# A SwiGLU output product by Strassen's scheme in a fused DeltaNet and FFN kernel

## The chip, the core and the metric

The kernel runs on one core of a Trainium2 chip. The metric is the device time of one execution in microseconds, lower is better. A core has five engines, each with its own in-order queue: TensorE (PE, matmuls, with the weight load PEld beside it), VectorE (DVE), ScalarE (ACT), GpSimd (POOL) and SyncE (SP, which issues most transfers). They wait for one another by semaphores. SBUF is the on-chip memory; PSUM has eight banks of 128 x 512 fp32 numbers, which matmuls write and VectorE and ScalarE read.

## The reference

Two blocks follow one another. The first is a DeltaNet recurrence over q, k, v of shape 4 x 8 x 768 x 48 (batch, heads, tokens, head width); the second is a SwiGLU feed-forward net on 3072 tokens of width 384 with 1536 hidden columns.

```python
k_n = k / (np.linalg.norm(k, axis=-1, keepdims=True) + 1e-06)
for t in range(S):
    kt, vt, bt = (k_n[:, :, t], v[:, :, t], beta[:, :, t, None])
    y[:, :, t] = np.einsum('bhd,bhde->bhe', q[:, :, t], state)
    v_old = np.einsum('bhde,bhd->bhe', state, kt)
    state = state + bt[:, :, :, None] * np.einsum('bhd,bhe->bhde', kt, vt - v_old)
# x: y as (tokens, heads * width)
rms = np.sqrt(np.mean(x * x, axis=-1, keepdims=True) + 1e-06)
xn = x / rms * rms_g
g = xn @ w_gate
silu = g * (1.0 / (1.0 + np.exp(-g)))
val = xn @ w_val
return (silu * val @ w_out).astype(np.float32)
```

Weights arrive as 64-bit floats and are turned into fp32 on the chip, with work on VectorE, ScalarE and, for the first nine of them, TensorE.

## The kernel before

The 768 tokens are cut into 12 chunks of 64; with four batches a chunk has 256 tokens for the feed-forward net. Per chunk the work is in three parts.

- *prep*: normalised keys are turned (L379) and multiplied with themselves (scores, L402, into kk through L500); the blocks go to DRAM and back into `at`, GpSimd scales and combines them (L519, L543, L553, L548), and fifteen solver steps on VectorE (`step`, L565 and L571) invert 32 x 32 triangles inside `acc`. ScalarE copies the result into `x` (L588), GpSimd a turned one into `xtr` (L592), and both go through DRAM into `mt`, `x2bd` and `m1bd`; two matmul groups (`merge1` L646 into `zz`, `merge2` L668) join two triangles into `mt`.
- *recur*: `ks` (L706) and VectorE's subtraction (L714) give `r`, `mr` (L739) gives `u` (L790, L792), `qs` (L752) and `pu` (L769) give the output, `ku` (L872) the update that VectorE adds to the state `sbd` (L881). The output is normalised into `yn` (L812, root on GpSimd L822, L827), turned (`xtr`, L837), scaled into `xf` (L840), and seven VectorE additions (L858) form sums of its blocks. `qpart` prepares the masked scores `pt`: ScalarE copies them (L445), GpSimd multiplies with the mask (L446).
- *ffn*: chunks 0 and 1 use `ffn_plain` (up L920, down L902). From chunk 2 on the gate and value products are 15 block products per half of the hidden columns instead of 18 (L1013), with weight sums made once by `factors` (L976, L978); ScalarE copies (L1025) or VectorE adds (L1023) collect them, then silu (L1029) and the product with the value (L1030) give `hf`, the 1536 hidden columns for 256 tokens. The output product runs over all 12 blocks of `hf` for both halves of tokens: 24 matmuls of 384 columns into two banks (`down_mm`, L902). `finish` copies both banks to `o_buf` (L894), and four transfers store them.

Python plans the order of the whole program ahead. `P.add` takes each operation with its engine, an estimated duration, a priority and the buffers that it reads and writes; `P.run` lets the ready operation that can start first go next, and among equals the lower priority value. Priorities come from `due(c, lead)`, a due time per chunk that moves by `PERIOD`. TensorE work of prep and recur is put ahead of the net's by `P.lead`. The order so found is each engine's queue, and the hardware keeps it whatever the real durations are. While TensorE would be idle in the first 70 us of the plan, a filler of matmuls without use is inserted (L1083).

Of the kernel before, what the change touches and what calls it, by code (L numbers as in the profile page):

```python
# [16 lines left out]
C = 64  # L17
W = 32
DP = 64
ENGINES = ("PE", "ACT", "DVE", "POOL", "SP")  # L20
# [16 lines left out]
class Plan:  # L37
# [3 lines left out]
    def __init__(self):  # L41
        self.ops, self.wrote, self.read, self.slack, self.lead = [], {}, {}, 0.0, 0.0

    def add(self, eng, dur, fn, prio, r=(), w=(), lat=0.15, ps=(), last=()):
# [11 lines left out]
        op.ahead, op.n = ahead, len(self.ops)  # L56
# [12 lines left out]
    def run(self, free, filler=None, until=0.0):  # L69
        at = dict.fromkeys(ENGINES, 0.0)  # L70
        cand = {e: [] for e in ENGINES}
        for op in self.ops:
            if not op.left:
                cand[op.eng].append(op)
        done, server = 0, 0.0
# [46 lines left out]
def kernel(  # L122
# [51 lines left out]
    o_buf = sbt("o_buf", [128, 768])  # L174
# [4 lines left out]
    NK, NKQ, NKK, NMT = 2, 2, 2, 2  # L179
# [8 lines left out]
    kk = sbt("kk", [128, 16, C], NKK)  # L188
# [4 lines left out]
    x = sbt("x", [128, W // 2, W])  # L193
    xt_ = sbt("xtr", [128, W, W // 2])
    m1bd = sbt("m1bd", [128, 16, 2, W])
    x2bd = sbt("x2bd", [128, 8, 4, W])
    zz = sbt("zz", [128, 4, 2, W])
    mt = sbt("mt", [128, 16, C], NMT)
# [5 lines left out]
    yn = sbt("yn", [128, 2, DM])  # L204

# [5 lines left out]
    sil = [tmp[:, a, 0:TOK] for a in range(2)]  # L211
# [3 lines left out]
    cvb = [o_buf, more[:, 4608:5376]]  # L215
    o_sb = o_buf.rearrange("p (two n) -> p two n", two=2)
# [19 lines left out]
    PERIOD = 54.5  # L236
# [6 lines left out]
    def setup():  # L243
# [32 lines left out]
        for i in range(NMT):  # L276
            P.add("POOL", 1.0, lambda t=mt[i]: nc.gpsimd.memset(t, 0.0), 1, w=[("mt", i, h_, bb) for h_ in range(3) for bb in range(2)] + [("mt", i, h_, bb, g) for h_ in range(2) for bb in range(2) for g in range(2)])

    def load_small():
        for i in range(8):  # L280
            src = beta.rearrange("b (y g) (c i t) -> i g (b y) c t", i=2, g=2, t=W)[i // 2 % 2, i % 2]
            dma(beta_b[16 * i : 16 * i + 16], src, 0.5, w=[("beta", i)], work=0.2)
        dma(g_sb, moe_rms_g.rearrange("(t p) -> p t", p=128), 1, w=["g"], after=30.0)


    def weights():
        todo = []
        for half_ in range(2):
# [6 lines left out]
            for f in range(6 * half_, 6 * half_ + 6, 2):  # L295
                src = moe_w_out[f * 128 : f * 128 + 256, :].rearrange("(a p) c -> p a c", a=2)
                todo.append((wo_sb[:, f : f + 2].rearrange("p a c -> p (a c)"), src, [("wo", f), ("wo", f + 1)]))
        for n, (dst, src, keys) in enumerate(todo):
# [7 lines left out]
            cc = cvb[a]  # L306

# [25 lines left out]
            P.add("DVE", 0.56, s4, pr, r=[("cvw", n)], w=[("o", a)])  # L333
            P.add("DVE", 0.97, s5, pr, r=[("raw", i)], w=[("o", a)])
            done = []
            if n < NPE:
                for x_ in range(2):
# [7 lines left out]
                    P.add("PE", 1.5, s6, pr, r=[("o", a), ("cvw", n), "ident"], w=[("cvp", n, x_)], ps=ps)  # L345
                    done.append(("cv", n, x_))
                    P.add("ACT", 0.48, lambda dst=dst[:, cols], ps=ps: nc.scalar.copy(dst, ps.t[:, 0:384]), pr, r=[("cvp", n, x_), ("cvw", n)], w=[done[-1]], last=ps)
            else:
                done.append(("cv", n))
                P.add("DVE", 0.97, lambda dst=dst, cc=cc: nc.vector.tensor_tensor(out=dst, in0=dst, in1=cc, op=ALU.add), pr, r=[("o", a)], w=[("cvw", n), done[-1]])  # L350
# [100 lines left out]
    def prep(c):  # L451
# [7 lines left out]
        i2, ikq, ikk, imt = c % 2, c % NKQ, c % NKK, c % NMT  # L459
# [5 lines left out]
        kkall = [("kk", ikk, d) for d in range(2)]  # L465
# [32 lines left out]
        for d in range(2):  # L498
            if c or d == 0:
                P.add("ACT", A(512), lambda d=d, ps=ps: nc.scalar.mul(kk[ikk][:, d:16:2], heads(ps[d]), -1.0), pr, r=[ps[d]], w=[("kk", ikk, d)], last=ps[d])  # L500
            else:
                P.add("DVE", V(512), lambda d=d, ps=ps: nc.vector.tensor_scalar_mul(kk[ikk][:, d:16:2], heads(ps[d]), -1.0), pr, r=[ps[d]], w=[("kk", ikk, d)], last=ps[d])

        kb, kbkeys = (kk[ikk], kkall) if c else (kraw, [("kr", d) for d in range(2)])
        dk = dkk[c % 2]
        for g in range(2):
            for i in range(2):
                r0 = 64 * g + W * i
                src = kb[r0 : r0 + W, :, W * i : W * i + W]
# [28 lines left out]

        diag = at_.rearrange("p j t -> p (j t)")[:, 1 : 1 + 66 * 15 + 1 : 66]
# [17 lines left out]
        P.add(e_, 0.69 if early else 1.3, share1, pi, r=[("at", 0), ("at", 1)], w=["x"])  # L557
        P.add(e_, 0.5, share3, pi, r=[("at", 0), ("at", 1)], w=["acc"])
        P.add(e_, 0.69 if early else 1.3, share2, pi, r=["x"], w=[("at", 0), ("at", 1)])
# [30 lines left out]
        P.add("ACT", 0.8, lambda: spread(x, nc.scalar.copy, False), pi, r=["acc"], w=["x"])  # L590
        if not early:
            P.add("POOL", 1.2, lambda: spread(xt_, lambda d, t: nc.gpsimd.tensor_copy(out=d, in_=t), True), pi, r=["acc"], w=["xtr"])  # L592
        q_ = "SP" if c else "ACT"
        for par in range(2):
            dst = dx[i2].rearrange("i g x (s two) t -> two (i g x) s t", two=2)[par]
            dma(dst, x[64 * par : 64 * par + 64], pi, r=["x"], w=[("dx", i2, par)], dur=0.63, work=1.0, eng=q_)
# [3 lines left out]
            dma(dst, xt_[64 * par : 64 * par + 32], pi, r=["xtr"], w=[("dxt", i2, par)], dur=0.65, work=1.0)  # L600
# [42 lines left out]
        def merge1():  # L643
            for b in range(B):
                for y_ in range(4):
                    nc.tensor.matmul(  # L646
                        ps1.t[W * y_ : W * y_ + W, 64 * b : 64 * b + 64],
                        kk[ikk][:, 4 * b + y_, W:C],
# [3 lines left out]
        P.add("PE", 0.7, merge1, pi, r=kkall + [("m1bd", g, bb) for g in range(2) for bb in range(2)], w=[ps1, "zz"], ps=ps1)  # L652
        if early:
            P.add("ACT", A(256), lambda: nc.scalar.copy(zz.rearrange("p b g s -> p (b g s)"), ps1.t[:, 0:256]), pi, r=[ps1], w=["zz"], last=ps1)
        else:
# [4 lines left out]
            ), pi, r=[ps1], w=["zz"], last=ps1)  # L660
# [13 lines left out]
        P.add("PE", 1.1, merge2, pi, r=["zz"] + [("x2bd", y_) for y_ in range(4)], w=ps2 + [("mt", imt, 2, bb) for bb in range(2)], ps=ps2)  # L674
# [10 lines left out]
    def recur(c):  # L685
        pr = due(c, 40)
        py = due(c, 30)
        ikq, imt, i2 = c % NKQ, c % NMT, c % 2
# [116 lines left out]
        px = py if c < 2 else due(c, 16)  # L805
        xdst, xkeys = (xp1, [("x1", p) for p in range(2)]) if c == 1 else (xf, [("xp", p) for p in range(2)])
        for h in halves:
# [24 lines left out]
            for p in h:  # L832
# [12 lines left out]
                ), px, r=[psx, "g"], w=[xkeys[p]], last=psx)  # L845
        if c > 1:
            X = lambda a, n, step=1: xf[:, a : a + step * (n - 1) + 1 : step]
            for dst, a, b_, op, n in (
# [11 lines left out]
                ), px, r=[("xp", 0)], w=["xc", ("xp", 1)])  # L860
# [25 lines left out]
    def finish(c, po, f0, f1):  # L886
        for p in range(2):
# [3 lines left out]
            if f0:  # L891
                P.add("DVE", V(384), lambda p=p: nc.vector.tensor_tensor(out=o_sb[:, p], in0=part[c][:, p], in1=po[p].t[:, 0:DM], op=ALU.add), -1, r=["po"] + partkeys[c], w=[("ob", p)], last=po[p])
            else:
                P.add("ACT", A(384), lambda p=p: nc.scalar.copy(o_sb[:, p], po[p].t[:, 0:DM]), -1, r=["po"], w=[("ob", p)], last=po[p])  # L894
            for bb in range(2):
                tok = (2 * bb + p) * S + c * C
                dma(out[tok : tok + C, :], o_sb[64 * bb : 64 * bb + 64, p], -1, r=[("ob", p)], w=[("out", c, p, bb)])

    def down_mm(po, f, f0, f1):
        def mm():  # L900
            for p in range(2):
                nc.tensor.matmul(  # L902
                    po[p].t[:, 0:DM], hf[:, f, 128 * p : 128 * p + 128], wo_sb[:, f], start=(f == f0), stop=(f == f1 - 1),
# [5 lines left out]
    def ffn_plain(c, f0, f1, start):  # L909
# [3 lines left out]
        def up(f):  # L913
            ps = Group()
            h_, i_, n = f // 6, f % 6 // 2, 128 * (f % 2)
            for side, key in enumerate(("wg", "wv")):
# [8 lines left out]
                P.add("PE", 1.31, mm, start + 3.9 * (f - f0), r=xk + [("wuse", h_)] + ready[(key, h_)], w=[ps, (("tmp", f % 2), ("hf", f, 0))[side]], ps=ps)  # L925
            a = f % 2
            P.add("ACT", A(256), lambda ps=ps: nc.scalar.activation(out=sil[a], in_=ps.t[:, 0:TOK], func=ACTF.Silu), -1, r=[ps], w=[("tmp", a)], last=ps)
            P.add("DVE", V(256), lambda ps=ps: nc.vector.tensor_tensor(out=hf[:, f], in0=sil[a], in1=ps.t[:, TOK : 2 * TOK], op=ALU.mult), -1, r=[("tmp", a), ps], w=[("hf", f, 0), ("hf", f, 1)], last=ps)

        def down(f):  # L930
            if f == f0:
                P.add("PE", 0.0, lambda: None, start, r=xk + [("cvp", n, x_) for n in range(NPE) for x_ in range(2)], w=["po"], ps=po[1])
            P.add("PE", 1.31, down_mm(po, f, f0, f1), start + 3.9 * (f - f0) + 9, r=[("hf", f, 0), ("hf", f, 1)] + ready[("wo", f)], w=["po"], ps=po[0])
# [66 lines left out]
    def ffn(c, start):  # L1000
        n = 0
        for h in range(2):
            ps = [Group() for _ in range(3)]
            for m, ((kind, slot), xs, b_, begin, o, more_, end) in enumerate(PRODUCTS):
# [21 lines left out]
                if end:  # L1026
# [4 lines left out]
                        out=hf[:, f0 : f0 + 2, 128 * p : 128 * p + 128],  # L1031
# [3 lines left out]
        po = [Group(), Group()]  # L1035
# [81 lines left out]
```

## Time and profile before

| what | value |
|---|---|
| median of 3 runs | 762.07 us (762.03 to 762.45) |
| profiled execution, its own time | 761.53 us |
| its span | 759.8 us |
| PE busy, share | 742.2 us, 98% |
| DVE busy, share | 528.9 us, 70% |
| ACT busy, share | 291.9 us, 38% |
| POOL busy, share | 194.1 us, 26% |
| gate and value matmuls, L1013 | 304.6 us |
| output matmuls, L902 | 197.1 us |

The span runs from the first to the last instruction that the profile shows; the execution's time has some 1.7 us around it. Busy time is a union, and matmuls are pipelined, so the mean duration of one matmul is longer than the spacing of two in a row; the chain that ended last shows spacings. PE is busy from 130.1 us on without an idle stretch up to the last output matmul. A fp32 matmul is two records in the profile.

### The profile page before, as it was taken

The numbers are of one execution on the slowest core, as the hardware profiler recorded it, in microseconds if no ns is written. First come the engines' busy times: TensorE is split into PE (matmuls) and PEld (weight loads), VectorE is DVE, ScalarE is ACT, GpSimd is POOL, SyncE is SP. The second block draws the span as 40 slices with busy tenths as digits, with TensorE's granted clock in tenths as the row PEclk, the third lists the DMA queues.
The fourth block names the chain that finished last, engine by engine and source line by source line (L and its number), as shares of the span: only waits on it lengthen the run. The fifth ranks groups of instructions, "written<-read, shape, count | busy, mean of one in ns | idle before, by whom it ended". The sixth has DMA issues, their size and how long they took to land.

```text
span 759.8 us, 21394 instructions
## 1 busy us (share of the span) xinstructions
PE 742.2 (98%) x9178; PEld 621.2 (82%) x9178; DVE 528.9 (70%) x1051; ACT 291.9 (38%) x698; POOL 194.1 (26%) x197
## 2 busy tenths in 40 slices
PE   9999995999999999999999999999999999999997
PEld 8877774877789789789699699699699699698894
DVE  4999999993865875865865865865955955944360
ACT  3425444123334334344344344344344254234230
POOL 5102206033222232332233233223323313200000
PEclk9999998999999999999999999999999999999999
DMA  7848386042352242242252252251251341120000
GB/s 169 211 88 239 108 221 154 1 70 45 63 91 45 44 79 55 43 83 52 43 89 47 43 92 43 44 92 43 49 86 44 58 77 44 21 51 3 21 2 21
DMA packets 206991, 54.55 MB, mean 72 GB/s; under 512 B 199216, under 2 KB 202288, under 8 KB 206896
## 3 DMA queue, kind: packets, MB, share of 16 engines
q1 hardware_dynamic: 201552, 52.19, 32.6%
q10 hardware_dynamic: 5344, 0.98, 0.8%
q8 instruction: 72, 1.18, 0.7%
q14 instruction: 23, 0.19, 0.1%
HBM read 40.83 MB, written 12.32 MB: 70 GB/s over the span
## 4 chain that ended last, share of the span: by engine, by line
PE 87%; DVE 4%; POOL 1%; issue 1%; ACT 0%; DVEq 0%
PE bank L1013 36%; PE bank L902 25%; PE bank L920 8%; PE bank L402 3%; PE bank L379 2%; PE bank L752 2%; PE bank L706 2%; PE bank L739 2%; PE bank L769 2%; PE bank L668 2%; PE bank L872 1%; PE bank L837 1%; PE bank L646 1%; DVE acc L571 1%; PE bank L1083 1%
## 5 line engine op out<-in xcount | busy, mean ns | idle before, releaser
L1023 DVE TENSOR_TENSOR tmp<-tmp,bank 128x512 f32<-128x512 f32 x180 | 123.1, 686 | 123.6 <-PE bank L1013 101.1
L902 PE MATMUL bank<-wo_sb,hf 128*128 128x384 f32 x576 | 197.1, 490 | 0.0
L1013 PE MATMUL bank<-xf,w_in 128*128 128x128 f32 x1440 | 179.5, 276 | 0.0
L1013 PEld LDWEIGHTS bank<-xf,w_in 128*128 128x128 f32 x1440 | 169.3, 192 | 2.8 <-issue 0.4
L902 PEld LDWEIGHTS bank<-wo_sb,hf 128*128 128x128 f32 x576 | 106.0, 190 | 63.7 <-issue 0.2
L1013 PE MATMUL bank<-xf,more 128*128 128x128 f32 x960 | 125.1, 277 | 0.0
L1013 PEld LDWEIGHTS bank<-xf,more 128*128 128x128 f32 x960 | 115.8, 192 | 4.6 <-DVE tmp L1023 1.4
L1029 ACT ACTIVATE tmp<-tmp 128x256 f32<-128x256 f32 x120 | 50.1, 417 | 116.1 <-DVE tmp L1023 115.8
L1025 ACT COPY tmp<-bank 128x512 f32<-128x512 f32 x120 | 69.9, 585 | 54.6 <-PE bank L1013 50.4
L571 DVE TENSOR_REDUCE acc<-acc 128x30 f32<-128x90 f32 (+4 forms) x180 | 85.0, 472 | 6.2
L519 POOL TENSOR_TENSOR at<-at,beta_b 128x1024 f32<-128x1024 f32 x10 | 23.6, 2362 | 203.9 <-DMA at<-dkk 203.8
L1030 DVE TENSOR_TENSOR hf<-tmp 128x256 f32<-128x256 f32 x120 | 58.7, 490 | 24.2 <-ACT tmp L1029 21.8
L565 DVE TENSOR_TENSOR acc<-acc,at 128x60 f32<-128x60 f32 (+4 forms) x180 | 68.6, 381 | 5.7
L422 POOL TENSOR_TENSOR knrm<-ksum,half 128x16 f32<-128x16 f32 x12 | 36.1, 3006 | 39.4 <-DVE ksum L421 39.2
L588 ACT COPY x<-acc 128x256 f32<-128x256 f32 x24 | 10.1, 431 | 91.4 <-DVE acc L571 90.7
L920 PE MATMUL bank<-xp,w_in 128*128 128x256 f32 x144 | 35.6, 398 | 6.6 <-DVE xp L840 6.6
L1083 PE MATMUL bank<-ident 128*128 128x128 f32 x314 | 39.0, 284 | 1.4 <-POOL ident masks.py:199 1.4
L1083 PEld LDWEIGHTS bank<-ident 128*128 128x128 f32 x314 | 37.3, 198 | 2.0 <-POOL ident masks.py:199 1.4
L920 PEld LDWEIGHTS bank<-xp,w_in 128*128 128x128 f32 x144 | 28.4, 200 | 12.9 <-DVE xp L840 6.8
L446 POOL TENSOR_TENSOR pt<-pt,mask_p 128x512 f32<-128x512 f32 x20 | 28.8, 1458 | 34.3 <-ACT pt L445 34.3
L881 DVE TENSOR_TENSOR sbd<-sbd,bank 64x384 f32<-64x384 f32 x40 | 22.1, 552 | 21.2 <-PE bank L872 20.7
L592 POOL COPY xtr<-acc 128x128 f32<-128x128 f32 x40 | 16.2, 448 | 73.5 <-DVE acc L571 73.5
(136 smaller groups left out, 873.6 us busy)
## 6 DMA issues: line engine op xcount, KB each, us to landing
at<-dkk SPq DMA_DIRECT2D x23, 256.0 KB, 4.1
more<-in_moe_w_gate_dram SPq DMA_DIRECT2D x6, 768.0 KB, 5.9
q<-in_q_dram SPq DMA_DIRECT2D x24, 192.0 KB, 4.5
more<-in_moe_w_val_dram SPq DMA_DIRECT2D x6, 768.0 KB, 5.2
vt<-in_v_dram SPq DMA_DIRECT2D x24, 192.0 KB, 4.1
more<-in_moe_w_out_dram SPq DMA_DIRECT2D x6, 768.0 KB, 6.5
out_dram<-o_buf SPq DMA_DIRECT2D x48, 96.0 KB, 2.2
k<-in_k_dram SPq DMA_DIRECT2D x23, 192.0 KB, 4.0
```

The costliest lines, as they stand in the source:

```text
L422: P.add("POOL", 2.95, lambda: nc.gpsimd.tensor_tensor(out=knrm[i2], in0=ksum[i2], in1=half, op=ALU.pow), pn, r=[("ksum", i2), "half"], w=[ ...
L446: P.add("POOL", 1.3, lambda dst=dst: nc.gpsimd.tensor_tensor(out=dst, in0=dst, in1=mask_p[:, None, :].to_broadcast([128, 8, C]), op=ALU.mu ...
L565: nc.vector.tensor_tensor(out=acc[:, 1:3, 0:n, j + 2 : W].rearrange("p a i t -> p i a t"), in0=acc[:, old, 0:n, j : j + 2, None].to_broadc ...
L571: nc.vector.tensor_reduce(out=acc[:, new, 0:n, j + 2 : W], in_=acc[:, lo : lo + 3, 0:n, j + 2 : W].rearrange("p a i t -> p i t a"), axis=A ...
L902: nc.tensor.matmul(po[p].t[:, 0:DM], hf[:, f, 128 * p : 128 * p + 128], wo_sb[:, f], start=(f == f0), stop=(f == f1 - 1), skip_group_check ...
L920: nc.tensor.matmul(ps.t[:, TOK * side : TOK * side + TOK], w_in[:, side, h_, 3 * t + i_, n : n + 128], x_[:, 2 * t : 2 * t + 2].rearrange( ...
L1013: nc.tensor.matmul(g.t[:, 128 * z : 128 * z + 128], fac[:, side, 128 * f : 128 * f + 128], xf[:, xs], start=(begin and z == 0), stop=False ...
L1023: P.add("DVE", V(512), lambda t=t, g=g: nc.vector.tensor_tensor(out=t, in0=t, in1=g.t, op=ALU.add), -1, r=[g], w=[tk], last=g)
L1025: P.add("ACT", A(512), lambda t=t, g=g: nc.scalar.copy(t, g.t), -1, r=[g], w=[tk], last=g)
L1029: P.add("ACT", A(256), lambda t=t: nc.scalar.activation(out=t[:, 0:256], in_=t[:, 0:256], func=ACTF.Silu), -1, w=[tk])
L1030: P.add("DVE", V(256), lambda t=t, f0=f0, p=p: nc.vector.tensor_tensor(out=hf[:, f0 : f0 + 2, 128 * p : 128 * p + 128], in0=t[:, 0:256].re ...
L1083: nc.tensor.matmul(warm[:, 0:128], ident, ident)
```

## The change

From chunk 2 on the output product is done as a 2 x 2 block product by seven block products. `hf` is split in two halves of tokens and two of hidden columns, `w_out` in two halves of hidden rows and two of output columns. `out_factors` makes three sums of weight blocks into a new buffer `wsum` once and overwrites one block of `w_out`; `down` makes four sums of `hf` blocks on VectorE per chunk, runs the seven products of six matmuls of 192 columns in three banks, and collects them with ScalarE copies and VectorE adds. `spot` orders the blocks of `hf` so that four of six in a half are complete before the last pair.

Room for `wsum` comes from buffers that are shared or dropped: `x` and `xtr` lie inside `acc`, `zz` inside `yn`, `kk` keeps one copy of its first part and two of its second, from chunk 2 on there is one `mt`, chunk 1's `kk`, `mt` and `x` lie inside `wsum`, `o_buf` is gone (outputs go from `tmp` and `part`), and chunk-1 sums use the old places.

The planner gets a backward pass: operations marked late take their priority from the operations that use them, less their own stretched duration. `recur` is entered before `prep`, `PERIOD` is 52.5 for 54.5, prep's slack is 0.6 for 1.5, and the priorities of the scaling into `xf` and of its sums are 29 us earlier.

```diff
+STRETCH = {"PE": 1.5, "ACT": 1.5, "DVE": 1.4, "POOL": 1.2, "SP": 1.0}
...
+        for op in reversed(self.ops):
+            if op.late:
+                op.prio = min(
+                    (u.prio - (0.0 if u.eng == op.eng and not op.dma else op.lat + u.slack + 0.2) for u in op.users),
+                    default=op.prio,
+                ) - STRETCH[op.eng] * op.dur - (3.0 if op.dma else 0.0)
...
-    o_buf = sbt("o_buf", [128, 768])
-    NK, NKQ, NKK, NMT = 2, 2, 2, 2
+    NK, NKQ = 2, 2
+    wsum = sbt("wsum", [128, 3, FT // 2, DM // 2])
+    wflat = wsum.rearrange("p a f n -> p (a f n)")
-    kk = sbt("kk", [128, 16, C], NKK)
+    kk3 = sbt("kk", [128, 3, 16, W])
+    kk = [kk3[:, 0:2], kk3[:, 0:3:2], wflat[:, 0:1024].rearrange("p (i x t) -> p i x t", i=2, t=W)]
-    x = sbt("x", [128, W // 2, W])
-    xt_ = sbt("xtr", [128, W, W // 2])
+    xs_ = [acc[:, 1], wflat[:, 2048:2560].rearrange("p (i t) -> p i t", t=W), wflat[:, 2560:3072].rearrange("p (i t) -> p i t", t=W)]
+    xt_ = acc[:, 2].rearrange("p i t -> p (i t)").rearrange("p (k i) -> p k i", i=W // 2)
-    zz = sbt("zz", [128, 4, 2, W])
-    mt = sbt("mt", [128, 16, C], NMT)
+    mt = [sbt("mt", [128, 16, C]), wflat[:, 1024:2048].rearrange("p (x t) -> p x t", t=C)]
+    zz = yn[:, 0, 0:256].rearrange("p (b g s) -> p b g s", b=4, g=2)
+    o_sb = [tmp[:, 3 + p, 0:DM] for p in range(2)]
...
-    PERIOD = 54.5
+    PERIOD = 52.5
...
+    def spot(f):
+        return f // 6 * 6 + (0, 1, 4, 5, 2, 3)[f % 6]
...
+        pxv = px if c < 2 else due(c, 45)
...
-        po = [Group(), Group()]
-        for f in range(FT):
-            P.add("PE", 1.31, down_mm(po, f, 0, FT), start + 29 + 1.4 * f, r=[("hf", f, 0), ("hf", f, 1)], w=["po"] + (["acq"] if f == 0 else []), ps=po)
-        finish(c, po, 0, FT)
+        down(c, start + 27.5)
+
+    def out_factors():
+        b = lambda i, j: wo_sb[:, 6 * i : 6 * i + 6, 192 * j : 192 * j + 192]
...
+        for n, (dst, in0, in1) in enumerate((
+            (wsum[:, 0], b(0, 1), b(0, 0)),
+            (wsum[:, 1], b(1, 1), wsum[:, 0]),
+            (wsum[:, 2], b(1, 0), wsum[:, 1]),
+            (b(0, 1), b(1, 1), b(0, 1)),
+        )):
+            P.add("DVE", V(1152), lambda dst=dst, in0=in0, in1=in1: nc.vector.tensor_tensor(out=dst, in0=in0, in1=in1, op=ALU.subtract), 175.0 if n == 3 else 165.0, r=wk, w=old + ["wsum"] + (["wouse"] if n == 3 else []))
+
+    def down(c, start):
+        a = lambda i, j: hf[:, 6 * j : 6 * j + 6, 128 * i : 128 * i + 128]
...
+        s1 = xp1
+        s2 = tflat[:, 512:1280].rearrange("p (f n) -> p f n", f=6)
+        p1, u2, p5 = tmp[:, 0, 0:192], tmp[:, 0, 192:384], tflat[:, 1280:1472]
...
+                for f in range(6):
+                    nc.tensor.matmul(g.t[:, 0:192], a_[:, f], b_[:, f], start=(begin and f == 0), stop=(f == 5), skip_group_check=True)
...
+        for z0, z1 in ((0, 4), (4, 6)):
+            k = ("x1", z0 // 4)
+            sums(s1, a(1, 0), a(1, 1), ALU.add, ak(1, 0, z0, z1) + ak(1, 1, z0, z1), [k], z0, z1)
+            sums(s2, s1, a(0, 0), ALU.subtract, ak(0, 0, z0, z1) + [k], s2k, z0, z1)
+        s1k = [("x1", 0), ("x1", 1)]
+        product(x, a(0, 0), ak(0, 0), b(0, 0), True, 0)
+        snap(p1, x, [("tmp", 0)])
+        product(z_, a(0, 1), ak(0, 1), b(1, 0), True, 2)
+        add(0, 0, p1, z_, [("tmp", 0)])
+        product(y, s1, s1k, wsum[:, 0], True, 4)
+        snap(p5, y, ["p5"])
+        sums(a(1, 0), a(0, 0), a(1, 0), ALU.subtract, ak(0, 0), ak(1, 0), 0, 6)
+        product(x, s2, s2k, wsum[:, 1], False, 6)
+        snap(u2, x, [("tmp", 0)])
+        sums(s1, a(0, 1), s2, ALU.subtract, ak(0, 1) + s2k, s1k, 0, 6)
+        product(y, s1, s1k, b(1, 1), False, 8)
+        add(0, 1, u2, y, [("tmp", 0)])
+        store(0)
+        product(x, a(1, 0), ak(1, 0), b(0, 1), False, 10)
+        add(1, 1, p5, x, [("tmp", 2), "p5"])
+        product(x, a(1, 1), ak(1, 1), wsum[:, 2], False, 12)
+        P.add("ACT", A(192), lambda: nc.scalar.copy(o_sb[1][:, 0:192], x.t[:, 0:192]), -1, r=[x], w=[("tmp", 4)], last=x)
+        store(1)
...
     for c in range(NCH):
-        P.slack, P.lead = 0.0 if c < 1 else 1.5, 1000.0
-        if c + 1 < NCH:
-            prep(c + 1)
-        P.slack = 0.0 if c < 1 else 0.3
-        recur(c)
...
+        for part_ in (recur, prep):
+            P.late = c + (part_ is prep) > 1
+            if part_ is prep:
+                P.slack, P.lead = 0.0 if c < 1 else 0.6, 1000.0
+                if c + 1 < NCH:
+                    prep(c + 1)
+            else:
+                P.slack, P.lead = 0.0 if c < 1 else 0.3, 1000.0
+                recur(c)
...
+            out_factors()
         elif c > 1:
             ffn(c, due(c, 0))
```

The seven products are called P1 to P7 below in the order of the code, and the matrix of `product(x, s2, ...)` is P4.

## The prediction

> **What bounds the kernel now.** I read the engine shares first, then the busy time by stage over three steady chunks, then the chain that ended last inside one chunk, and last the VectorE and GpSimd timelines of that chunk. The engine line of the page:
>
> ```profile
> PE 742.2 (98%) x9178; PEld 621.2 (82%) x9178; DVE 528.9 (70%) x1051; ACT 291.9 (38%) x698; POOL 194.1 (26%) x197
> ```
>
> The stage table (stretch, its length, then busy us of PE, PEld, DVE, ACT, POOL) for two chunks in the middle:
>
> ```profile
> 384.83:440.64 55.81, 55.81 (x744) 47.47 (x744) 39.04 (x81) 23.57 (x57) 17.07 (x18) 1.00 0.32 61
> 440.64:496.44 55.80, 55.80 (x744) 47.46 (x744) 38.53 (x81) 23.58 (x57) 17.06 (x18) 1.00 0.33 61
> ```
>
> TensorE never waits: a steady chunk costs 55.81 us, all of it matmul. VectorE is busy 38.8 of that. The chain inside a chunk is TensorE alone:
>
> ```profile
> 384.83 8.04 PE bank L1013 x72
> ...
> 419.58 0.93 PE bank L872 x64
> 420.51 1.02 PE bank L379 x8
> 421.54 2.58 PE bank L902 x8
> 424.12 1.09 PE bank L402 x64
> 425.21 1.49 PE bank L902 x4
> 426.70 0.66 PE bank L837 x6
> 427.36 10.32 PE bank L902 x32
> ```
>
> A matmul leaves two records. 72 records of 128 columns take 8.04 us, 0.1117 each; 32 of 384 columns 10.32, 0.3225 each; elsewhere in the chain 12 of 256 columns take 2.59, 0.2158 each. A piece after the small L402 matmuls is 0.20 longer (1.49, not 1.29). VectorE in the same place:
>
> ```profile
> 414.61 1.76 DVE L1030 TENSOR_TENSOR hf<-tmp 128x256 f32<-128x256 f32 x1
> ...
> 420.56 2.27 DVE L881 TENSOR_TENSOR sbd<-sbd,bank 64x384 f32<-64x384 f32 x4 [1.28 <-PE bank L872]
> 422.87 0.22 DVE L565 TENSOR_TENSOR acc<-acc,at 128x60 f32<-128x60 f32 x1
> ...
> 426.82 0.79 DVE L565 TENSOR_TENSOR acc<-acc,at 128x240 f32<-128x240 f32 x1
> ...
> 431.86 0.41 DVE L565 TENSOR_TENSOR acc<-acc,at 128x240 f32<-128x240 f32 x1
> ...
> 437.98 1.02 DVE L840 TENSOR_TENSOR xf<-bank,g_sb 128x384 f32<-128x384 f32 x2
> 438.92 2.41 DVE L858 TENSOR_TENSOR xf<-xf 128x256 f32<-128x256 f32 x7
> ```
>
> The fifteen solver steps (L565, L571) fill 422.87 to 436.87 without a gap, exactly under the output product, which today asks nothing of VectorE. Two rows are odd: 1.76 us for a product that mostly takes 0.42, and 0.79 where the same shape takes 0.41. GpSimd explains both:
>
> ```profile
> 414.35 1.75 POOL L543 TENSOR_TENSOR x<-at 128x512 f32<-128x512 f32 x1
> ...
> 425.91 2.83 POOL L446 TENSOR_TENSOR pt<-pt,mask_p 128x512 f32<-128x512 f32 x2 [3.55 <-ACT pt L445]
> ```
>
> [...] L1030 (two SBUF inputs) ends when L543 ends, while L1023, which reads a bank, keeps 0.69 beside L519. [...] the trace has 0.686 for N=512 [...] and 0.957 for 768 [...]
>
> **The change, part by part.** *Output product.* Before, 24 matmuls of 384 columns: 48 x 0.3225 = 15.48 us. After, seven products P1 to P7 of six matmuls of 192 columns: 84 records. No row has 192 columns; the middle of 128 and 256 is 0.1638 [...]. 84 x 0.1638 = 13.76. Saved 1.72 a chunk, 17.2 over chunks 2 to 11. The other TensorE work of a chunk is the same, and the built queue has as many switches from small matmuls as before. New TensorE bound: 54.1 a chunk.
>
> *ScalarE.* Two copies of 0.48 go, four of 192 columns come (estimate 0.33 each, from the 128x192 L812): +0.36 on an engine busy 23.6 of 55.8.
>
> *VectorE, each chunk.* Sums of 512 (two, 0.69), 256 (two, 0.42), 768 (two, 0.96) and three adds of 192 from a bank (0.36 [...]): 5.2 us, so 44.0 of 54.1. As an average that fits. But all except the 512 pair fall into the stretch that the solver already fills.
>
> *That stretch, worked.* Clock 0 is the start of L872. The built TensorE queue from there: ku 0.93, q transposes 1.02, P1 1.97, last gate product 0.89, scores 1.09, P2 0.20+1.97, xtr 0.66, P3 1.97, P4 1.97: P5 could start at 12.67. It waits for the second s1 on VectorE, whose queue now reads: one state add 0.57 (from 0.98), steps 1 to 5 3.95, a bank add 0.65, step 6 0.98, hf 0.40, s1 and s2 tails 0.34+0.42, add 0.30, A10 difference 0.90, L840 pair 0.94, one combination 0.42, s1 0.92 (spacings, a little under durations). Sum 10.79, end 11.77: 0.9 us of cover. On to the next chunk's L706, which waits for the last state add: TensorE 12.67 + P5, P6 3.94 + two gate products 1.79 + P7 1.97 + ten gate products 8.93 = 29.3. VectorE 11.77 + combinations 1.9 + steps 7 to 15 8.3 + two adds 0.6 + norm sums 1.2 + four bank adds and an hf 2.9 + three state adds 1.7 + norms 0.5 = 28.9. So VectorE is continuously busy for 28 us and just keeps up.
>
> [...] The mask pair (2.83 us) follows the scores of the q part as before. In the built ScalarE queue its copy now stands behind the P1 copy, the yn scaling and the last silu, so GpSimd begins near 7.25 and ends near 10.1. Then the two tails (two SBUF inputs) are due at 7.5: each finds a mask running, and the second ends near 10.35 instead of 8.3. That adds up to 2.05: P5 waits 1.2, and L706 1.75. If the masks fall beside the reductions or bank adds, nothing. Stall s per chunk from 0 to 1.75; I take 1.0, since solver steps next to the pair lost only 0.38 each before.
>
> *Chunk by chunk.* Chunks 3 to 9: 7 x (1.72 - 1.0) = 5.0. Chunk 2: its seven products follow each other behind the last gate product with only xtr between; add, silu, hf need about 1.8 us beyond that cover, which eats its gain: 0. Chunk 10 has no solver under it: 1.7. Chunk 11: P2 waits for hf about 1.3 at the end: 0.4. Sum 7.1.
>
> *Outside the loop.* Four subtractions of 1152 columns (1.36 each [...], 5.4) go to VectorE near 165 to 215, busy 38.0 of 54.5 there: hidden, at worst 3 us if they delay a first gate product. The one large TensorE wait before is
>
> ```profile
> PE bank L920 <- DVE xp L840: 6.6, 1, 6.6
> ```
>
> The L840 pair now stands before one conversion add (1.93) but behind a norm sum and reciprocal (about 1.6): -0.3, between -2 and +2, taken as 0. First-chunk output adds: the same count.
>
> *Buffers, at nothing.* x and xtr inside acc make the next memset of acc wait for their stores; the next use of acc is some 30 us later. One mt: its reload follows the solver, over 20 us after L739 read it. zz inside yn: zz is consumed near 408, yn written at 419.6. Output tiles inside tmp: a store lands in 2.2 us, tmp 3 is rewritten six or more products later. SP issues as many output DMAs as before. If one of these covers failed, the wait would show before L1025 or L524. Later due times only reorder; the built queue is what I costed.
>
> **Sum.** Span 759.8 - 7.1 = 752.7; the profiled execution took 761.5, and the median is 762.07, so about 755.
>
> **Rivals.** *No stall*: the masks miss the tails and VectorE keeps its 0.3 us. For it: [...] 762 - 17 = 745. *Break-even*: s of 1.75 in seven chunks leaves 0.2 + 2.1 = 2: 760 to 763. *Slower, VectorE becomes the bound*: at the same place, P5 and L706, with the first-half sums also caught: the 512 pair and the last hf multiplications stand among L519, L543 and L548 (about 6 us of GpSimd that read SBUF), so the queue enters the stretch late. It decides from s = 1.72 + 2.1/7 = 2.0; s = 2.7 gives 7 x 1.0 - 2.1 = +5, 767. For it: the 1.76 row. Against: before L872 VectorE waited 1.28, and 3.2 before 412.29. *The seven products do not run at 0.164 a record*: the weight load of a record must hide under 0.164; it hides under 0.112 at 128 columns, so against.
>
> **Numbers.** No stall 0.27, main case (748 to 760) 0.40, break-even 0.11, slower 0.22. A difference of 0.2%, 1.5 us, is about what can be told from none. Faster 0.67, same 0.11, slower 0.22. Range 744 to 767; the main case's own is 748 to 760.
>
> **What would show it.** In the stage table a middle chunk near 55.1 with TensorE busy 54.1; in the waits the output product waiting for VectorE's sums and L706's successor for the state add; product records of 0.16 spacing. [...] Wrong if TensorE waits mostly for banks or ScalarE, if records are 0.18 (saving gone), or if early chunks lose several us at the hand-over to chunk 2.

## The result and the profile after

The changed kernel takes 754.62 us, the median of 4 runs (754.26 to 754.70), against 762.05 us before (761.30 to 762.45): 0.9903 of the time before, 95% interval 0.9886 to 0.992. The forecast was 755. The profiled span went from 759.8 to 752.8 us. The engine line of the page after:

```profile
PE 728.9 (97%) x9538; PEld 670.5 (89%) x9538; DVE 588.6 (78%) x1145; ACT 293.6 (39%) x718; POOL 194.0 (26%) x197
```

TensorE is busy 13.3 us less, though it runs 360 more records; VectorE is busy 59.7 us more. The stage table of two steady chunks, from the start of one seventh product to that of the next (stretch, its length, then busy us of PE, PEld, DVE, ACT, POOL, the granted clock, the DMA share, GB/s):

```profile
436.58:491.66 55.08, 54.22 (x781) 52.32 (x780) 44.96 (x90) 23.38 (x59) 17.12 (x17) 1.00 0.33 62
491.66:546.73 55.07, 54.21 (x781) 52.31 (x780) 44.70 (x90) 23.50 (x59) 17.10 (x17) 1.00 0.32 62
```

A chunk now takes 55.07 us where it took 55.81, and for the first time TensorE is not busy all through: 54.22 of 55.08. The waits of TensorE (engine and line, what it waited for, us in all, times, longest) name where:

```profile
PE bank L940 <- DVE xp L863: 6.7, 1, 6.7
PE bank L1089 <- DVE xp L1082: 5.0, 6, 0.9
PE bank L1089 <- DVE hf L1050: 2.1, 2, 1.1
```

L1089 are the matmuls of the seven products, L1082 the sums of `hf` blocks. The first line is the old wait of the first chunk (6.6 before). The other two are new; the third belongs to chunks 2 and 11, whose second product waits for `hf`. The chain that ended last, for the chunk that corresponds to the one shown of before (start, us, what):

```profile
424.62 1.39 DVE xp L1082
...
426.04 1.38 DVE tmp L1082
...
429.81 0.88 DVE xp L1082
...
430.82 4.14 PE bank L1089 x24
...
436.75 1.95 PE bank L1089 x12
```

Before, this chain was TensorE alone. Now it passes through VectorE in front of the fifth product. The last line gives the price of a product: 12 records in 1.95 us, 0.1625 each. VectorE in the same place (start, us, line, operation, output and input):

```profile
424.17 0.42 DVE L1050 TENSOR_TENSOR hf<-tmp 128x256 f32<-128x256 f32 x1
424.62 1.38 DVE L1082 TENSOR_TENSOR xp<-hf 128x256 f32<-128x256 f32 x1
426.04 1.38 DVE L1082 TENSOR_TENSOR tmp<-xp,hf 128x256 f32<-128x256 f32 x1
...
429.74 0.94 DVE L1082 TENSOR_TENSOR xp<-hf,tmp 128x768 f32<-128x768 f32 x1
```

The two tail sums take 1.38 us where the same shape takes 0.42 one line above. GpSimd, and TensorE's fifth product:

```profile
424.33 2.80 POOL L464 TENSOR_TENSOR pt<-pt,mask_p 128x512 f32<-128x512 f32 x2 [4.12 <-ACT pt L463]
```

```profile
430.82 2.19 PE L1089 MATMUL bank<-wo_sb,xp 128*128 128x192 f32 x12 [0.86 <-DVE xp L1082]
```

The mask pair runs from 424.33 to 427.13, two masks of 1.39 and 1.45. Each tail ends 0.28 after a mask: the first at 426.00 against 425.72, the second at 427.41 against 427.13. The second sum then ends at 430.68 and the fifth product begins at 430.82. It could have begun at 429.80, for the fourth begins at 427.85 and a product takes 1.95: it is 1.02 late. The recorded wait is 0.86, because a record of 192 columns lasts 0.33 by the profile while the next follows 0.16 after its start, and idle time is counted from the modelled end of the last record.

Only chunks 5 to 9 lose both tails in this way. In chunks 3 and 4 the pair is over before the tails (it begins at 313.73 and 368.66), and one other VectorE instruction with two SBUF inputs is caught beside it, 0.95 and 1.27 us instead of 0.42. The fifth product waits 0.41 and 0.68 there. Chunks 10 and 11 have no mask pair under their products and no such wait.

### The profile page after: what moved, and what is told of

Read it like the earlier page. It is cut to its first block, busy times and chain, and to the rows that moved or that the text cites. A ratio compares the mean times of both kernels' runs of the same rounds, so it can differ in the third digit from the quotient of the medians.

```text
span 752.8 us, 22292 instructions
## 1 busy us (share of the span) xinstructions
PE 728.9 (97%) x9538; PEld 670.5 (89%) x9538; DVE 588.6 (78%) x1145; ACT 293.6 (39%) x718; POOL 194.0 (26%) x197
## 4 chain that ended last, share of the span: by engine, by line
PE 79%; DVE 18%; issue 2%; POOL 1%; ACT 0%; DVEq 0%; POOLq 0%
PE bank L1033 35%; PE bank L1089 12%; PE bank L940 7%; PE bank L1179 5%; PE bank L922 3%; DVE acc L593 3%; PE bank L420 2%; DVE acc L587 2%; PE bank L728 2%; PE bank L397 2%; PE bank L774 2%; DVE xp L1082 2%; DVE tmp L1043 2%; PE bank L761 2%; PE bank L690 1%
## 5 line engine op out<-in xcount | busy, mean ns | idle before, releaser
L1033 PE MATMUL bank<-xf,w_in 128*128 128x128 f32 x1440 | 187.1, 278 | 0.4 <-issue 0.4
L1033 PEld LDWEIGHTS bank<-xf,w_in 128*128 128x128 f32 x1440 | 172.1, 192 | 5.1 <-issue 2.0
L1033 PE MATMUL bank<-xf,more 128*128 128x128 f32 x960 | 122.9, 276 | 0.3 <-DVE tmp L1043 0.3
L593 DVE TENSOR_REDUCE acc<-acc 128x30 f32<-128x90 f32 (+4 forms) x180 | 85.0, 472 | 6.2
L1050 DVE TENSOR_TENSOR hf<-tmp 128x256 f32<-128x256 f32 x120 | 62.3, 527 | 28.2 <-ACT tmp L1049 27.1
L587 DVE TENSOR_TENSOR acc<-acc,at 128x60 f32<-128x60 f32 (+4 forms) x180 | 63.6, 353 | 7.7 <-POOL at L570 4.4
L1089 PE MATMUL bank<-wo_sb,hf 128*128 128x192 f32 x360 | 64.2, 328 | 2.1 <-DVE hf L1050 2.1
L1089 PEld LDWEIGHTS bank<-wo_sb,hf 128*128 128x128 f32 x360 | 58.3, 190 | 2.9 <-DVE hf L1050 2.5
L922 PE MATMUL bank<-wo_sb,hf 128*128 128x384 f32 x96 | 35.2, 495 | 0.0
L940 PE MATMUL bank<-xf,w_in 128*128 128x256 f32 x144 | 33.8, 382 | 0.0
L940 PEld LDWEIGHTS bank<-xf,w_in 128*128 128x128 f32 x144 | 27.0, 190 | 5.8 <-issue 0.2
```

The source lines that it names most:

```text
L587: nc.vector.tensor_tensor(out=acc[:, 1:3, 0:n, j + 2 : W].rearrange("p a i t -> p i a t"), in0=acc[:, old, 0:n, j : j + 2, None].to_broadc ...
L593: nc.vector.tensor_reduce(out=acc[:, new, 0:n, j + 2 : W], in_=acc[:, lo : lo + 3, 0:n, j + 2 : W].rearrange("p a i t -> p i t a"), axis=A ...
L922: nc.tensor.matmul(po[p].t[:, 0:DM], hf[:, spot(f), 128 * p : 128 * p + 128], wo_sb[:, spot(f)], start=(f == f0), stop=(f == f1 - 1), skip ...
L940: nc.tensor.matmul(ps.t[:, TOK * side : TOK * side + TOK], w_in[:, side, h_, 3 * t + i_, n : n + 128], x_[:, 2 * t : 2 * t + 2].rearrange( ...
L1033: nc.tensor.matmul(g.t[:, 128 * z : 128 * z + 128], fac[:, side, 128 * f : 128 * f + 128], xf[:, xs], start=(begin and z == 0), stop=False ...
L1050: P.add("DVE", V(256), lambda t=t, f0=f0, p=p: nc.vector.tensor_tensor(out=hf[:, spot(f0) : spot(f0) + 2, 128 * p : 128 * p + 128], in0=t[ ...
```

## The experiments

**Is it the masks?** The theory: the mask pair on GpSimd and the two tails on VectorE hold each other off, which costs about 1 us a chunk. The rival: VectorE has no time left here, masks or not. Two kernels take the masks away from the tails, in two ways. e1 doesn't issue them from chunk 2 on (the plan is unchanged; it leaves out the multiplication by the causal mask):

```diff
-                P.add("POOL", 1.3, lambda dst=dst: nc.gpsimd.tensor_tensor(
-                    out=dst, in0=dst, in1=mask_p[:, None, :].to_broadcast([128, 8, C]), op=ALU.mult,
-                ), pr, r=["mask"], w=[("pt", d)])
+                P.add("POOL", 1.3, lambda: None, pr, r=["mask"], w=[("pt", d)])
```

> The changed kernel with the two GpSimd mask multiplications per chunk left out from chunk 2 on (the scores keep what lies above the diagonal); plan and every other queue are unchanged. [...] the two sum tails go from 1.39 us back to about 0.40 each, the fifth product no longer waits 0.86 us for the second s1, a middle chunk goes from 55.07 to 54.2, and the time from 754.6 to about 749.5 (748.5 to 750.5). Rival, VectorE's queue is simply too full there: the tails are not what holds it, the wait stays over 0.5 us and the time at 753 or more.

e2 does all the work, but issues each pair later, just ahead of GpSimd's next clearing of `acc`:

```diff
+    held = []
...
+                def masked(dst=dst):
+                    nc.gpsimd.tensor_tensor(out=dst, in0=dst, in1=mask_p[:, None, :].to_broadcast([128, 8, C]), op=ALU.mult)
...
+                P.add("POOL", 1.3, (lambda m=masked: held.append(m)) if c < NCH - 1 else masked, pr, r=["mask"], w=[("pt", d)])
...
         def start():
+            while held:
+                held.pop(0)()
             nc.gpsimd.memset(acc[:, 0:4:3], 0.0)
```

> The changed kernel with the same work, but each mask pair is issued later on GpSimd, just ahead of the next memset of acc, some 23 us later, where VectorE mostly reads banks; all other queues are unchanged. [...] as without masks, about 749.5; up to 1 us more a chunk if the pair now holds hf multiplications that a gate product waits for, or delays the memset: 749 to 752. Rival, GpSimd's work costs the same wherever it stands, or the queue is too full: 753.5 to 756.

Measured: e1 747.30 us, 0.9797 of before (0.9776 to 0.9819); e2 747.81 us, 0.981 (0.9794 to 0.9827). Both are some 7 us faster than the changed kernel. In e2 the waits at the fifth product are gone except one of 0.9 us, in chunk 9: beside its products the mask pair of chunk 11 is still issued at once. The stage table of e2, between the same points of the chunk:

```profile
432.81:486.78 53.97, 53.97 (x781) 52.34 (x780) 43.41 (x90) 23.36 (x59) 16.94 (x17) 1.00 0.33 63
486.78:540.75 53.97, 53.97 (x781) 52.33 (x779) 42.86 (x90) 23.46 (x59) 16.95 (x17) 1.00 0.32 62
```

VectorE and TensorE of e2 in the first of these places:

```profile
421.94 0.42 DVE L1086 TENSOR_TENSOR xp<-hf 128x256 f32<-128x256 f32 x1
422.40 0.42 DVE L1086 TENSOR_TENSOR tmp<-xp,hf 128x256 f32<-128x256 f32 x1
...
425.37 0.96 DVE L1086 TENSOR_TENSOR xp<-hf,tmp 128x768 f32<-128x768 f32 x1
```

```profile
423.22 2.12 PE L1093 MATMUL bank<-wsum,xp 128*128 128x192 f32 x12
...
427.12 2.11 PE L1093 MATMUL bank<-wo_sb,xp 128*128 128x192 f32 x12
```

The tails are back at 0.42, with the same VectorE order around them; the second sum ends at 426.33, 0.79 before the fifth product begins, and TensorE is busy for the whole 53.97 us. That is the bound without a stall. The changed kernel's 55.07 is this plus 1.10, and the masks beside the tails are the whole of it: the fifth product is 1.02 late, and the sixth follows it after 2.03 us where 1.95 is usual. Since e2 computes everything and is faster than both kernels, the stall is not needed: the masks have the rest of the chunk to run in.

The first line of the second view shows what now sets the second sum's start. The sum overwrites the data of the third product, which is read up to 425.34 by the profile (423.22 + 2.12); the sum begins at 425.37, after VectorE was idle for 0.12.

**Do the masks cost anything by themselves?** The control holds them in the kernel before.

> The kernel before with its masks issued later in the chunk, ahead of the next clearing of the triangle buffers, and nothing else. Theory (the masks cost time only because VectorE's sums for the fifth product are on the path; the kernel before has no such sums): no change, 761.5 to 762.8 us. Rival (holding the masks helps by itself, whatever the output product): 755 to 758 us.

Measured: 762.38 us, ratio 1.0 (0.9991 to 1.0009). In the kernel before, whose output product needs no sums from VectorE, moving the masks changes nothing.

**Is the gain the seven products?** e3 is the changed kernel with the old product: the buffers, the order of planning and the new due times stay.

```diff
-        down(c, start + 27.5)
+        po = [Group(), Group()]
+        for f in range(FT):
+            P.add("PE", 1.31, down_mm(po, f, 0, FT), start + 29 + 1.4 * f, r=[("hf", f, 0), ("hf", f, 1)], w=["po"] + (["acq"] if f == 0 else []), ps=po)
...
-            out_factors()
```

> The changed kernel with the output product as before (24 matmuls of 384 columns in two banks, two ScalarE copies), without the weight sums; shared buffers and the backward priorities stay. Theory that the seven products carry the gain and the rest only reorders: TensorE work is that of before, 55.8 a chunk without waits, 760.5 to 763.5. Rival, buffers and new priorities carry it: 755 to 758.

Measured: 762.12 us, ratio 1.0002 (0.9991 to 1.0012). All the gain comes from the seven products; the rest of the change neither wins nor loses anything as built.

**How close is VectorE?** e4 computes the second sum of the fifth product's data twice, some 0.96 us more on VectorE in each of ten chunks.

```diff
-        sums(s1, a(0, 1), s2, ALU.subtract, ak(0, 1) + s2k, s1k, 0, 6)
+        sums(s1, a(0, 1), s2, ALU.subtract, ak(0, 1) + s2k, s1k, 0, 6, times=2)
```

> The changed kernel with the second s1 sum (768 columns) computed twice in a row in every chunk from 2 on, the plan not knowing of it. Theory that VectorE bounds the stretch under the output product: each of the chunks with a solver loses the whole 0.9 us at the fifth product, about 6 to 7 us in all, 760.5 to 762. Rival, the stretch has slack and the 0.86 us wait is a one-off of order: 754.6 to 756.5.

Measured: 763.35 us, the median of 20 runs from 761.06 to 766.56, ratio 1.0021 (1.001 to 1.0033), 8.7 us above the changed kernel and more than expected. The waits and the fifth product of a steady chunk in e4:

```profile
PE bank L1094 <- DVE xp L1085: 13.1, 10, 1.9
```

```profile
489.42 2.19 PE L1094 MATMUL bank<-wo_sb,xp 128*128 128x192 f32 x12 [1.84 <-DVE xp L1085]
```

All ten chunks wait, and a steady one takes 56.07 us, 1.00 more than in the changed kernel: while the masks are there, the whole added sum is lost. TensorE keeps the changed kernel's order of work through the longer waits (1.84 here, 0.86 there). A steady chunk's gain (55.81 to 55.07, 0.74) is less than one such sum. e8 does the same on top of e2.

> e2_masks_held with the second sum of the fifth product's data computed twice over (0.9 us more on VectorE in each of 10 chunks; same sum, same place). It measures the slack that VectorE has ahead of the fifth product once the masks are out of the way. Theory (the prediction's 0.9 us of slack, 0.9 us from the sum): nearly hidden, 0 to 2 us more than e2_masks_held, so 747.8 to 750 us, with waits of at most 0.2 us at the fifth product. Rival (no slack is left, VectorE is the bound with or without the masks): the whole 9 us more, 756 to 757 us.

Measured: 754.47 us, ratio 0.9894 (0.9878 to 0.991), 6.7 us above e2: far from the 0 to 2 of the theory, and not the 9 of the rival. The steady chunk:

```profile
431.20 2.19 PE L1098 MATMUL bank<-wo_sb,xp 128*128 128x192 f32 x12 [0.18 <-DVE xp L1089]
```

The chunk takes 54.40 us, 0.43 more than in e2, though the recorded wait is 0.18. The starts explain it: the doubled sum ends at 431.06, the fifth product begins at 431.20, 0.35 later than it could (428.90 + 1.95), and the sixth comes 0.08 later than usual behind it. So the slack for the sum is 0.65, not the 0.79 between its end and the product in e2, because a product begins 0.15 after the end of the sum that it waits for. And this slack is not VectorE's: the sum has to lie between the end of the third product and the start of the fifth. In chunk 11 VectorE is idle for 1.5 us before the sum, and the fifth product waits the same 0.18. The run so tells how long the sum may take, not how full VectorE's queue is.

The rest of the 6.7 is in chunks without that slack: chunk 2 waits 0.61, 3 waits 0.87, 4 waits 0.79, and the one whose masks are not held 1.83. Recorded waits add up to 5.2 us against 0.9 in e2, and nine more chunks now stop, each at some 0.24 beyond its recorded wait (0.16 that the wait leaves out, 0.08 behind the product): 4.3 + 2.2 = 6.5.

**The last mask pair.** e7 is e2 with chunk 11's pair held too, until after the turned copy of the solved triangle:

```diff
+            def turned():
+                spread(xt_, lambda d, t: nc.gpsimd.tensor_copy(out=d, in_=t), True)
+                while c == NCH - 1 and held:
+                    held.pop(0)()
```

> The changed kernel with the mask pairs of chunks 2 to 10 held as in e2_masks_held, and the pair of chunk 11 too, which there was still issued at once: it follows the turned copy of the solved triangle on GpSimd. Theory: the last wait of TensorE for the sums of the fifth product (0.9 us in e2_masks_held) goes and nothing takes its place: 746.5 to 747.3 us. Rival (the time of the last chunks is set by the chain of the recurrence, not by this wait): 747.5 to 748.2 us, as e2_masks_held.

Measured: 747.05 us (746.58 to 747.44), ratio 0.9796 (0.9782 to 0.9811), with no wait left for the sums of the fifth product. Its median lies 0.8 below e2, and its runs lie wholly below e2's. The medians alone would be weak, since the kernel before was 0.35 faster in e7's series than in e2's (761.95 and 762.30). The traces are clear: chunk 9 takes 53.97 us between the ends of two output products where it takes 55.11 in e2. It is the fastest kernel here that does the whole computation, 7.6 us below the changed one.

**What do the new due times do?** The prediction said that they only reorder. e5 puts the whole plan back, order of planning included, and keeps the products and the shared buffers.

> The seven products and the shared chunk buffers stay; the plan's period, slacks, priorities and the order of planning of the two parts of a chunk (the next chunk's preparation, then the recurrence) go back to those of the kernel before. Theory (the gain is the saved TensorE records less the waits that VectorE's sums leave, and the new plan only shifts which work meets those sums): within 4 us of the changed kernel on either side, so 751 to 759 us; TensorE's waits for the sums (line of the seven products) change by as much as the time does. Rival (the new due times carry the gain): 760 us or more, with waits outside the output product that the changed kernel doesn't have.

Measured: 1048.24 us, ratio 1.3758 (1.3719 to 1.3796). This run does not answer its question. With one `mt` and the preparation entered first, the plan makes a chunk's recurrence follow the next chunk's preparation and read that chunk's block, so it computes something else, and each chunk waits for transfers:

```profile
PE bank L668 <- DMA m1bd<-dxt: 180.2, 9, 22.6
```

It shows only that one `mt` requires the new order. e9 keeps that order and puts back the rest; e10 takes away only the backward pass:

```diff
-            if op.late:
+            if op.late and False:
```

> The changed kernel with its order of planning (recurrence, then the next chunk's preparation) and its shared buffers, but with the old period (54.5), the old slack of the preparation (1.5), the old due time of the copies after the recurrence and no priorities worked back from due times. This is what e5_old_plan was meant to ask. Theory (the gain is the saved TensorE records less the waits at the fifth product; the new due times only decide which VectorE work stands ahead of the sums): 752 to 760 us, and whatever differs from the changed kernel shows as waits of TensorE for VectorE or ScalarE in the output product and at the next chunk's first products. Rival (with one buffer where there were two, the old due times send the recurrence and the preparation into each other): 775 us or more, with TensorE waiting for the preparation's transfers as in e5_old_plan.

> The changed kernel without the priorities worked back from due times alone; period, slacks and order of planning as changed. Theory: 752 to 760 us, as e9_old_priorities or between it and the changed kernel. Rival: 775 us or more, which would put the need for the new due times on the shared buffers, whatever the period and slacks.

Measured: e9 803.41 us, ratio 1.0534 (1.0516 to 1.0551); e10 780.72, ratio 1.0236 (1.0219 to 1.0253). The theory fell in both: without the backward pass the change would have been a loss of 18 us, and without the rest of the new due times as well, of 41. In e9 TensorE's two largest waits are 28.3 us in 8 for the sums of the next chunk's `xf`, and 12.6 in 9 for adds at the output product. VectorE does the whole triangle before the next chunk's factor sums:

```profile
459.43 0.28 DVE L593 TENSOR_REDUCE acc<-acc 128x30 f32<-128x90 f32 x1
459.62 0.94 DVE L437 TENSOR_REDUCE ksum<-r 128x16 f32<-128x768 f32 x1
460.60 0.17 DVE L439 TENSOR_SCALAR ksum<-ksum 128x16 f32<-128x16 f32 x1
460.68 1.01 DVE L863 TENSOR_TENSOR xf<-bank,g_sb 128x384 f32<-128x384 f32 x2
461.62 2.63 DVE L881 TENSOR_TENSOR xf<-xf 128x256 f32<-128x256 f32 x7
```

```profile
462.50 1.49 PE L1033 MATMUL bank<-xf,more 128*128 128x128 f32 x8 [3.97 <-DVE xf L881]
463.78 4.16 PE L1033 MATMUL bank<-xf,w_in 128*128 128x128 f32 x24
```

L593 of 128x30 is the last solver step; L863 and L881 come only after it, and TensorE waits 3.97 us for the first of them. In the changed kernel the L863 pair begins at 428.47 and the solver's last step at 443.20: the steps fill the gaps behind it.

Behind the wait stands a second loss. The 24 records that follow take 4.16 us where 24 take 2.84 elsewhere in this chunk: from 463.12 to 466.53 the granted clock is 0.50, and the records follow each other at 0.214 us instead of 0.112. Each of e9's six waits of some 4 us has such a stretch (24 records behind it take 4.16 to 4.47), and there is a seventh in chunk 3, at a wait of 1.84 (4.47). They last 27.3 us together, of which TensorE idles 1.9; half of the rest, some 13 of the 41 us, is an estimate of what the clock costs. The mean granted clock of the profiled execution is 0.976, that of the changed kernel 0.995. The kernel before and the changed one have no such stretch between 135 us and the end of the last product.

e11 asks who needs that order, with e3's old product under e9's due times.

> e3_no_strassen (the old output product in the changed kernel) with the old period, slacks and due times of e9_old_priorities: fewer buffers are then all that is left of the change, beside the order of planning. It tells who needs the new priorities. If the shared buffers need them (the preparation, planned one buffer later, collides with the recurrence under the old due times): 785 us or more, with long waits of TensorE at the first products of the next chunk for VectorE's factor sums. If only the seven products need them (their 28.9 us of VectorE work leave no room for the triangle ahead of the next chunk): 760 to 768 us, without such waits.

Measured: 780.79 us, ratio 1.0243 (1.0225 to 1.0262), with this at the head of its waits:

```profile
PE bank L1033 <- DVE xf L881: 13.3, 5, 3.1
```

The four kernels together, medians in us:

| | old due times | new due times |
|---|---|---|
| old product, shared buffers | 780.79 (e11) | 762.12 (e3) |
| seven products, shared buffers | 803.41 (e9) | 754.62 (changed) |

The expectation named 785 or more for the shared buffers and 760 to 768 for the products; 780.79 is neither, but with the waits of the first. The shared buffers (with the new order of `hf`'s blocks and the outputs in `tmp`, which e11 keeps too) cost 18 us under the old due times, and the new ones win that back. The order of planning isn't the cause: entered in the new order, the kernel before has the same queue on every engine, instruction for instruction. Under the old due times the seven products cost 22.6 us more (803.41 against 780.79); under the new ones they gain 7.5. Which of the shared buffers costs the 18 us was not tried. Of the 18, 13.3 stand in that line of waits. Two stretches at a granted clock of 0.50, 3.41 us each and behind two of the five waits (24 records in 4.47 us behind one of them), account for another 3.4 by the same estimate.

## Why the prediction was right

The prediction's mechanism and its sum held, by its own steps. Times are on the clock of the prediction, from the start of L872 (now L895, 417.37):

| step | predicted | measured |
|---|---|---|
| TensorE work of a steady chunk | 54.1 | 53.97 (e2) |
| record of 192 columns | 0.1638 | 0.1625 |
| second sum ends, no masks | 11.77 | 11.64 (e2) |
| fifth product could start, by modelled ends | 12.67 | 12.59 |
| mask pair | 7.25 to 10.1 | 6.96 to 9.76 |
| second tail ends | 10.35 | 10.05 |
| stall of a chunk | 1.0, range 0 to 1.75 | 1.10, of it 0.86 recorded idle |
| chunks 3 to 9 | 5.0 | 5.2 |
| chunk 2, and all before it | 0 | -0.6 |
| chunk 10 | 1.7 | 1.06 |
| chunk 11 | 0.4 | 0.48 |
| behind the last product (outside the loop) | 0 | 0.8 |
| sum | 7.1 | 7.0 |

Chunk rows come from the ends of the output products in both traces (before 273.22, 663.62, 712.55 and 754.85 for chunks 2, 9, 10 and 11; after 273.80, 658.98, 706.85, 748.67).

*The hold-off* was read from two odd rows of the kernel before, and e1 and e2 show it: masks and tails apart, 53.97; together, 55.07. A tail takes 1.38 us beside a mask and 0.42 without one. What in the hardware holds the two off was not shown. One reading was a little off: L1030 of the kernel before does not end when L543 ends but 0.28 later (416.38 and 416.10), the same 0.28 as the tails. The prediction's 0.36 for the adds of 192 is what a solver step of that width takes in the kernel before (L565, 0.358, the mean of 24); its 1.36 for the subtractions of 1152 lies on the straight line through the 0.686 at 512 columns and the 0.957 at 768 there, an estimate. Measured were 0.34 to 0.35 and 1.35 to 1.36.

*The size of the stall* came out right partly by luck. The prediction had a range from 0 to 1.75 and took 1.0 because solver steps lost only 0.38 each, an analogy that did not say what two sums in a row would lose, 0.96 each. Its cover of 0.9 was also too large: the second sum may be 0.65 late (e8), because a product begins 0.15 behind its sum and because the clock's starts of TensorE are modelled ends, 0.16 after the real ones. Its longest case put a second loss at the next chunk's L706 (now L728); no wait is recorded there. Two slips of its sums change nothing: the break-even case needs -0.2 where it writes 0.2, and its own terms give a loss of 1.65 at L706, not 1.75.

*The cases.* "No stall, 745" is what e7 comes near to: 747.05. "It decides from s = 2.0": in e4 the stall is 56.07 - 53.97 = 2.10, and the time is 1.3 us above before. That is near the turning point, though not an exact test of it, since chunks 2, 10 and 11 stop in e4 as well.

*What was mis-sized.* The row of chunk 2 holds everything up to the end of its product. From the end of the old first wait (130.12 and 129.83) it is 143.10 us before and 143.97 after: chunk 2's saving is eaten by three waits that the kernel before lacks, 1.01 for `hf` at the second product, as said, and 0.36 and 0.35 at gate products. Half a microsecond in this row is still within its scatter, for in e2 and e7, whose work is the same up to there, the product ends at 272.24 and 273.37. The time from the last product to the end of the span fell from 4.97 to 4.17 us; the prediction had no term for it. These two cancel, which is luck.

The rows of chunks 10 and 11 are cut at the ends of output products, and the changed plan moves work across these cuts. Between the ends of chunks 9 and 10 the changed kernel does the 32 records of L728 (1.47 us), which the kernel before did ahead of the first cut (L706), and eight gate records (0.89) fewer. With that 0.58 put back, chunk 10 saves 1.64, close to the 1.7. Chunk 11 then loses 0.4 instead of gaining 0.4, since eight of its gate records were done ahead of its cut: beside the wait of 1.11 at its second product, which was foreseen, TensorE waits 0.45 at its seventh for the add of the sixth, which was not.

*What was wrong.* "Buffers at nothing" holds for the kernel as built (e3). But the covers named for it are those of the built queue, not of the buffers: with the old due times they cost 18 us (e11). And "Later due times only reorder" is true of the queues and misleading about the price: that reordering is worth 26 us by its backward pass alone (780.72 against 754.62) and 49 in all (803.41), the loss of clock included. The number came out right because the built queues were costed, not the diff.

## What to carry to other kernels

Saving TensorE work by giving sums to VectorE pays only as far as those sums are done in time at the one place where TensorE asks for them; an average of 44.8 busy in 55.1 us says nothing about that place. Before adding VectorE work with two SBUF inputs, look for GpSimd work at the same moment (a sum took 1.38 us beside a mask, 0.42 without), and try moving that to a stretch where VectorE is not on the path: here it doubled the gain, from 7.4 to some 15 us. When a change moves buffers and due times together, cost the built queue of each engine, for here neither part could be priced alone. And before asking whether an engine has time for a sum, look whether the sum's output is still being read: that, and not VectorE, set the slack of the second sum once the masks were moved.

## What the runs showed of the hardware

- At the fifth product TensorE began 0.14 to 0.15 us after the end of the VectorE sum that it waited for (chunks 3 to 9 of the changed kernel, steady chunks of e4 and e8). A stop cost what the product began late, and 0.08 more until the next product. The profile's wait leaves out 0.16 of the lateness, so the chunk grew by 0.24 to 0.25 more than the wait: 0.18 recorded and 0.43 in the period (e8), 0.86 and 1.10 (changed kernel), 1.86 and 2.10 (e4). A small lateness can leave no wait at all: in chunk 3 of e2 the fourth product begins at 317.13 and the fifth at 319.11, 0.03 late, and the sixth 2.03 after it.
- Two masks in a row held up two sums in a row. The first sum ended at 426.00, 0.28 after the first mask (425.72), and the next at 427.41, 0.28 after the second (427.13). Each sum took 0.96 us longer than without masks (1.38 for 0.42). The second mask took 1.45 us; beside at most one such instruction, in chunks 3 and 4, a mask took 1.27.
- A VectorE instruction that reads a bank for one of its inputs kept its time beside a mask: in chunk 4 the bank add of 512 columns took 0.68 and the two scalings into `xf` 0.55 each, while the `hf` product with two SBUF inputs took 1.27 instead of 0.42.
- At each wait of some 4 us in e9 the granted TensorE clock was 0.50 for 3.41 us (6.83 once), and 128-column records were spaced 0.214 instead of 0.112. A wait of 1.84 had such a stretch too, one of 2.52 had none (24 records in 2.84). Of the waits of 3.08 in e11 two had one and one had none. What sets the clock was not shown.
